# Decays loaded to every partition by their own transfer, and eight blank products in one run, at the start of a linear-attention and mixer kernel

## The chip, the cores and the metric

The kernel runs on one core of one Trainium2 chip. The metric is device time in microseconds for the whole program, the median of three runs. The profile is of one further execution of the same program; its span, from the first instruction to the last, is about one microsecond shorter than the measured time.

## What is computed

Two blocks follow each other. The first is linear attention with a decay per head: batch 4, 8 heads, 768 positions, head size 64, in blocks of positions.

```python
rel = pos[:, None] - pos[None, :]
Dmask = np.where(rel >= 0, lam[:, None, None] ** rel[None, :, :], 0.0)
for b in range(nb):
    intra = einsum('bhic,bhjc->bhij', qb, kb) * Dmask[None]
    intra = einsum('bhij,bhjd->bhid', intra, vb)
    inter = einsum('bhid,bhde->bhie', qb * lam_pow[None], kv_state)
    out[:, :, sl] = intra + inter
    kv_state = lam_block * kv_state + einsum('bhsd,bhse->bhde', kb * rev_pow, vb)
```

Everything that depends on the decays (`Dmask`, `lam_pow`, `rev_pow`, `lam_block`) is made from the eight numbers `lam`.

The second block takes the attention output as x (4 x 768 x 512), mixes positions through a product of rank 32, and applies a two-layer network of width 2048:

```python
h = xt @ U @ V
u = x + h.transpose(0, 2, 1)
ch = np.maximum(u @ w_ch1, 0.0) @ w_ch2
return u + ch
```

## The kernel before

The work is tiled by 128 positions: 24 tiles (four batches of six), called s in the code. The kernel uses its own block of 128 positions where the reference has 64, which gives the same result.

**The front**, about the first 115 us, goes through the tiles one after the other. The order is written out by hand: the list `pieces` names, for each tile, functions that each emit a few instructions, and the loop at the end of the set-up calls them in that order. An engine executes its instructions in the order in which they are emitted, so the list is also the order on every engine. For a tile these are:

- `prep`: TensorE transposes q and k (line 348) by a product with the identity, and ScalarE copies the result out of PSUM (line 351). For tile 0 this goes in two halves, q then k, and the first halves use the PSUM tags pq and pk, the second ones pt and pu. Afterwards `load_next` issues a later load of q and of k.
- `scale`: GpSimd multiplies q by powers of the decay (`powq`) and the next tile's k by `rev`.
- `scores`: TensorE multiplies q by k into PSUM tile `pss` (line 393), 16 passes.
- `masked`: VectorE multiplies `pss` by the decay mask into `sm` (line 402), two instructions.
- `inter` and `intra`: TensorE multiplies the state and the masked scores by v into `px` (lines 434 and 446); ScalarE copies `px` out.
- `state`: TensorE and VectorE update the running state (line 411 and after), and the next v is loaded.
- later ones for the mixer's rank-32 product (`low`, `mix`) and the transposes of its result (`turn`), and `aside`, which converts the weights.

The loads of q, k and v (line 272) come from HBM in rows of 256 B. A tile of each is 256 KB; three buffers hold q and v, four hold k. Almost all are issued by SyncE in the order of the calls; only the two halves of the first k are on ScalarE's queue. Tile 0's q and k come in two halves each.

**The hidden layers** follow, from about 115 us to the end: `hidden` (lines 722 and 732) and `product` (lines 855 to 859), long runs of 128x512 products with conversions on the other engines beside them.

**The set-up**, which the change touches, lies before the loop. `blank` is a tile of zeros. `keep_busy(n)` (line 336) makes n products of `blank` with itself, which nobody reads, into PSUM with tag pq. A product in fp32 is two passes of TensorE, each with its weight load. `lam_row` holds the eight decays and 128 ones on one partition. The product `pl` (line 670) of the ones and the decays puts the decays on all 128 partitions, and VectorE copies it into `lamb` (line 672). From `lamb`, `constants` makes the mask with eight scans (line 302) and `powers` makes `powq` with four (line 314); `rev` is a column of the mask (line 675). VectorE executes these in that order, and `masked(0)` after them.

The tile names in the profile are those of the code: `idle` is the output of the blank products, `pl` that of the ones product, `qraw`, `kraw` and `vraw` are loads.

Of the kernel before, what the change touches and what calls it, by code (L numbers as in the profile page):

```python
# [8 lines left out]
FP32 = mybir.dt.float32  # L9
# [5 lines left out]
P = 128  # L15
# [3 lines left out]
def kernel(  # L19
# [28 lines left out]
    nc = tc.nc  # L48

    B, H, S, D = q.shape  # L50
# [37 lines left out]
    def set_ends(t):  # L88
        nc.vector.memset(t[:, 0:1], 1151.0)
        nc.vector.memset(t[:, 1:2], 255.0 * (1 << 23))  # L90
        ends.append(t)
# [145 lines left out]
    consts = att_ctx.enter_context(tc.tile_pool(name="consts", bufs=1))  # L237
# [10 lines left out]
    def one_bank(shape, name, tag):  # L248
        return psf.tile(shape, FP32, tag=tag, name=name)
# [7 lines left out]
    lamb = consts.tile([P, H], FP32, name="lamb")  # L257
# [40 lines left out]
    def constants():  # L298
        for a in range(HP):
            for x in range(2):  # L300
                h = 2 * a + x
                nc.vector.tensor_tensor_scan(
                    mask[:, x, a, :], lamb[:, h : h + 1].broadcast_to([P, P]), ident, 0.0,
                    ALU.mult, ALU.add,
                )
# [26 lines left out]
    def keep_busy(n):  # L332

        out = one_bank([P, C], "idle", "pq")
        for i in range(n):
            nc.tensor.matmul(out=out[:, 0:P], lhsT=blank, rhs=blank, start=True, stop=True)  # L336
# [240 lines left out]
    def load_next(name, engine=nc.sync):  # L577
        if waiting[name]:
            load(name, waiting[name].pop(0), engine)
# [71 lines left out]

    ordered = ctx.enter_context(ExitStack())
    ordered.enter_context(tc.manual_schedule())
    lam_row = consts.tile([1, H + P], FP32, name="lam_row")
    blank = x_pool.tile([P, C], FP32, tag="x", name="blank")[:, 0:P]
    nc.vector.memset(blank, 0.0)
    nc.vector.memset(lam_row[:, H:], 1.0)
    set_ends(vp[:, S + C : S + C + 2].bitcast(FP32))
    nc.scalar.dma_start(out=lam_row[:, 0:H], in_=lam.unsqueeze(0))
    load_next("q", nc.sync)  # L660
    load_next("k", nc.scalar)
    for name in "qkvkv":
# [2 lines left out]
    for name in "qkv":  # L665
        load_next(name)
    make_identity(nc, ident)
    keep_busy(2)
    pl = one_bank([P, H], "pl", "pt")
    nc.tensor.matmul(out=pl, lhsT=lam_row[:, H:], rhs=lam_row[:, 0:H], start=True, stop=True)  # L670
    keep_busy(3)
    nc.vector.tensor_copy(out=lamb, in_=pl)
    constants()
    powers()
    nc.vector.tensor_copy(out=rev, in_=mask[:, :, :, P - 1])
# [282 lines left out]
```

## Time and profile before

| | |
|---|---|
| time, median of three (lowest, highest) | 673.5 us (673.49, 673.6) |
| span of the profile | 672.5 us |
| TensorE products busy | 665.9 us, 99% of the span |
| VectorE busy | 496.6 us, 74% |
| ScalarE busy | 278.7 us, 41% |
| GpSimd busy | 112.8 us, 17% |
| mean rate of the transfers | 195 GB/s; 208 to 239 GB/s in each of the first six of 40 slices |
| blank products, ten passes | 2.9 us busy, 1.05 to 4.38 us |
| scans for the mask, eight | 2.6 us busy, 0.40 us each |

How to read the lines shown later: in the chain of work and the timeline each line begins with the start in us and the duration in us, then the engine. "x6" is six instructions merged into one line, and the duration is that from the first start to the last end. In brackets stands how long the engine had been idle before, and what ended it. A busy TensorE is not a TensorE at its full rate: the same product can take twice as long at half the clock. SPq and ACTq are the queues on which SyncE and ScalarE issue transfers; the duration there is that of issuing, not of the transfer.

### The profile page before, as it was taken

How to read it: one execution, taken by the hardware profiler on the slowest of the kernel's cores; microseconds unless marked ns; L12 is line 12 of the kernel's file. 1: busy time of each engine (PE TensorE's matmuls, PEld its weight loads, DVE VectorE, ACT ScalarE, POOL GpSimd, SP SyncE). 2: the span in 40 equal slices, each digit the busy share in tenths (PEclk: the TensorE clock that was granted, in tenths of full speed). 3: DMA queues.
4: the chain of work that ended last, by engine and by line, in shares of the span. 5: the costliest groups of instructions: out<-in, count | busy, mean ns of one | idle time of the engine just before them, and what ended most of it. 6: DMA issues, size and time to landing. Idle time of an engine off the chain costs nothing.

```text
span 672.5 us, 13170 instructions
## 1 busy us (share of the span) xinstructions
PE 665.9 (99%) x5124; PEld 545.4 (81%) x5124; DVE 496.6 (74%) x873; ACT 278.7 (41%) x517; POOL 112.8 (17%) x92
## 2 busy tenths in 40 slices
PE   9999999999999999999999999999999999999997
PEld 8888898787888888888888888888888888888885
DVE  4679999777999777777797255786586775865854
ACT  4675767454555444444455121332232322322320
POOL 4455667340000000000000000030030200300300
PEclk9999999999999999999999999999999999999999
DMA  9999993264776555555587999854363363443421
GB/s 208 214 228 239 237 232 109 84 215 156 235 276 240 204 203 204 204 203 204 203 280 253 325 314 387 291 185 140 94 206 107 110 204 94 158 155 95 161 89 62
DMA packets 131775, 131.27 MB, mean 195 GB/s; under 512 B 81346, under 2 KB 89794, under 8 KB 131714
## 3 DMA queue, kind: packets, MB, share of 16 engines
q1 hardware_dynamic: 130656, 130.18, 61.3%
q8 instruction: 40, 0.66, 0.4%
q10 hardware_dynamic: 1058, 0.26, 0.2%
q14 instruction: 21, 0.17, 0.1%
HBM read 80.09 MB, written 50.33 MB: 194 GB/s over the span
## 4 chain that ended last, share of the span: by engine, by line
PE 96%; DVE 2%; ACT 2%; issue 0%; DVEq 0%; ACTq 0%
PE pz L722 27%; PE pz L857 13%; PE pd L732 13%; PE pz L855 13%; PE pd L859 13%; PE pss L393 3%; PE px L446 3%; PE put L523 2%; PE pq L348 2%; PE px L434 1%; PE pkv L411 1%; PE pk L348 1%; PE pp L461 1%; PE pu L506 1%; PE idle L336 0%; ACT qt L351 0%
## 5 line engine op out<-in xcount | busy, mean ns | idle before, releaser
L722 PE MATMUL pz<-u_hl,w 128*128 128x512 f32 x768 | 190.4, 397 | 0.0
L722 PEld LDWEIGHTS pz<-u_hl,w 128*128 128x128 f32 x768 | 144.0, 188 | 35.5 <-issue 0.4
L857 PE MATMUL pz<-w_hl,m 128*128 128x512 f32 x384 | 151.1, 396 | 0.0
L855 PE MATMUL pz<-w_hl,m 128*128 128x512 f32 x384 | 150.9, 396 | 0.0
L859 PE MATMUL pd<-w_d,m 128*128 128x512 f32 x384 | 149.5, 396 | 0.0
L838 ACT ACTIVATE m<-mt 128x512 fp32r<-128x512 f32 x96 | 60.7, 633 | 196.0 <-PE pd L859 141.7
L839 DVE SCALAR_TENSOR_TENSOR m<-rm,m 128x512 fp32r<-128x512 f32 x96 | 71.4, 745 | 52.2 <-ACT m L838 52.1
L884 POOL TENSOR_TENSOR o<-o,u 128x512 f32<-128x512 f32 x20 | 29.9, 1529 | 447.3 <-DVE o L880 447.3
L737 DVE SCALAR_TENSOR_TENSOR r<-pd,r 128x512 f32<-128x512 f32 x96 | 61.8, 685 | 54.0 <-ACT r L728 43.5
L732 PE MATMUL pd<-u_d,w 128*128 128x512 f32 x384 | 98.6, 397 | 0.0
L728 ACT ACTIVATE r<-pz 128x512 f32<-128x512 f32 x96 | 52.2, 596 | 93.6 <-PE pz L722 92.9
L857 PEld LDWEIGHTS pz<-w_hl,m 128*128 128x128 f32 x384 | 72.3, 188 | 17.7
L855 PEld LDWEIGHTS pz<-w_hl,m 128*128 128x128 f32 x384 | 72.3, 188 | 17.6
L859 PEld LDWEIGHTS pd<-w_d,m 128*128 128x128 f32 x384 | 72.3, 188 | 17.6
L732 PEld LDWEIGHTS pd<-u_d,w 128*128 128x128 f32 x384 | 72.1, 188 | 17.3
L840 DVE SCALAR_TENSOR_TENSOR m<-m 128x512 fp32r<-128x512 f32 x96 | 69.0, 720 | 0.9
L837 DVE TENSOR_SCALAR mt<-rm 128x512 uint32<-128x512 uint32 x96 | 46.1, 481 | 28.0 <-DMA rm<-r_d 27.6
L402 DVE TENSOR_TENSOR sm<-pss,mask 128x512 f32<-128x512 f32 x48 | 30.8, 683 | 7.4 <-PE pss L393 7.3
L205 ACT CAST w<-wt 128x512 fp32r<-128x512 f32 x32 | 19.9, 622 | 30.5 <-DVE wt L202 23.4
L376 POOL TENSOR_TENSOR qs<-qt,powq 128x512 f32<-128x512 f32 x20 | 25.9, 1296 | 23.3 <-ACT qt L351 22.3
L446 PEld LDWEIGHTS px<-vraw,sm 128*64 128x64 f32 x768 | 24.7, 137 | 6.0 <-issue 2.4
L446 PE MATMUL px<-vraw,sm 128*64 128x64 f32 x768 | 28.3, 226 | 0.5 <-DVE sm L402 0.4
(88 smaller groups left out, 682.7 us busy)
## 6 DMA issues: line engine op xcount, KB each, us to landing
r_d<-r SPq DMA_DIRECT2D x96, 256.0 KB, 2.5
rm<-r_d SPq DMA_DIRECT2D x96, 256.0 KB, 2.7
words<-in_moe_w_ch_dram SPq DMA_DIRECT2D x30, 512.0 KB, 4.4
w_d<-w SPq DMA_DIRECT2D x16, 768.0 KB, 3.3
w_hl<-w_d SPq DMA_DIRECT2D x16, 512.0 KB, 6.2
vraw<-in_v_dram SPq DMA_DIRECT2D x24, 256.0 KB, 4.6
u_d<-x_nat SPq DMA_DIRECT2D x24, 256.0 KB, 3.5
u<-u_d SPq DMA_DIRECT2D x24, 256.0 KB, 4.1
```

Source lines behind the costliest of these rows:

```text
L446: nc.tensor.matmul(out=px[half[t], x, a, :], lhsT=sm[:, x, a, half[t]], rhs=vr[:, 2 * a + x, :], start=(first and a == 0), stop=(a == HP - 1),
L722: nc.tensor.matmul(out=acc[g][0], lhsT=w[:, n, ct, :], rhs=uhl[g][:, n, ct, :], start=(ct == 0 and n == 0), stop=(ct == CT - 1 and n == 1),)
L728: nc.scalar.mul(rs[g], acc[g][0], 4096.0 + 1.0)
L732: nc.tensor.matmul(out=acc[g][1], lhsT=w[:, 2, ct, :], rhs=ud[g][:, ct, :], start=(ct == 0), stop=(ct == CT - 1),)
L737: nc.vector.scalar_tensor_tensor(rs[g], acc[g][1], 4096.0, rs[g], ALU.mult, ALU.add)
L837: nc.vector.tensor_scalar(t.bitcast(U32), r.bitcast(U32), HI, None, ALU.bitwise_and)
L838: nc.scalar.activation(out=m[:, 0], in_=t, func=AF.Relu)
L839: nc.vector.scalar_tensor_tensor(m[:, 1], r, 0.0, hi, ALU.max, ALU.subtract)
L840: nc.vector.scalar_tensor_tensor(m[:, 2], hi, E, low, ALU.mult, ALU.subtract)
L855: nc.tensor.matmul(out=pz, lhsT=m[:, 0, cols], rhs=hl[:, 0], start=first, stop=False)
L857: nc.tensor.matmul(out=pz, lhsT=m[:, 1, cols], rhs=hl[:, 1], start=False, stop=end)
L859: nc.tensor.matmul(out=pd, lhsT=m[:, 2, cols], rhs=dd, start=first, stop=end)
```

## The change

The decays are sent to all 128 partitions by the transfer itself, which reads the eight numbers once for each partition and writes them straight into `lamb`. The tile `lam_row`, the filling of its ones, the product `pl` and the copy out of PSUM go. The blank products were two, then the ones product, then three; they become eight in one run. What they are for is to keep TensorE at work from its first microsecond until the first data are there. Nothing else is edited; the order of the loads is as before.

```diff
     ordered.enter_context(tc.manual_schedule())
-    lam_row = consts.tile([1, H + P], FP32, name="lam_row")
     blank = x_pool.tile([P, C], FP32, tag="x", name="blank")[:, 0:P]
     nc.vector.memset(blank, 0.0)
-    nc.vector.memset(lam_row[:, H:], 1.0)
     set_ends(vp[:, S + C : S + C + 2].bitcast(FP32))
-    nc.scalar.dma_start(out=lam_row[:, 0:H], in_=lam.unsqueeze(0))
+    nc.scalar.dma_start(out=lamb, in_=lam.unsqueeze(0).broadcast_to([P, H]))
     load_next("q", nc.sync)
     load_next("k", nc.scalar)
...
     make_identity(nc, ident)
-    keep_busy(2)
-    pl = one_bank([P, H], "pl", "pt")
-    nc.tensor.matmul(out=pl, lhsT=lam_row[:, H:], rhs=lam_row[:, 0:H], start=True, stop=True)
-    keep_busy(3)
-    nc.vector.tensor_copy(out=lamb, in_=pl)
+    keep_busy(8)
     constants()
     powers()
     nc.vector.tensor_copy(out=rev, in_=mask[:, :, :, P - 1])
```

## The prediction

> **What bounds the kernel now.** I read the page first: busy shares, the slices, the chain that ended last.
>
> ```profile
> DMA  9999993264776555555587999854363363443421
> ...
> PE 96%; DVE 2%; ACT 2%; issue 0%; DVEq 0%; ACTq 0%
> ```
>
> The chain is TensorE nearly everywhere, and the list of waits between 110 us and the end shows only nine waits of TensorE, the longest 0.4 us. So a shift of TensorE's work at the start should reach the end almost unchanged, unless something in the front takes it back. The slices name the candidate: the DMA engines are full in the first six slices, about 100 us. Next, the chain in order of time for the first microseconds:
>
> ```profile
> 0.83 0.18 DVE blank L656
> ...
> 1.05 1.23 PE idle L336 x4
> 2.28 0.52 PE pl L670 x2
> 2.80 1.58 PE idle L336 x6
> 4.38 0.10 issue
> 4.48 0.66 PE pq L348 x2
> ...
> 6.42 2.01 PE pss L393 x16
> ...
> 11.32 1.09 PE pss L393 x16
> ```
>
> The blanks and the ones product fill TensorE to 4.38; the first transposes follow 0.10 us later. Each fp32 blank is two passes (five blanks are ten passes). The first scores take 2.01 us, the second, same shapes, 1.09: the first ran at half the rate. The single pass starts show where this changes: start to start a 128-column pass takes 0.21 us up to 8.85 us and 0.11 us after. The trace's record of the granted clock begins its full interval at 8.885 us and ends it at 671.07: 662.19 us, which is 194 times 3.413. Then the timeline of the start, where VectorE and the loads can be seen:
>
> ```profile
> 2.83 0.17 DVE L672 COPY lamb<-pl 128x8 f32<-128x8 f32 x1 [1.69 <-PE pl L670]
> 3.11 2.63 DVE L302 TENSOR_TENSOR_SCAN mask<-lamb,ident 128x128 f32<-128x128 f32 x8
> ...
> 7.33 0.14 DVE L675 COPY small<-mask 128x8 f32<-128x8 f32 x1
> ...
> 8.48 1.29 DVE L402 TENSOR_TENSOR sm<-pss,mask 128x512 f32<-128x512 f32 x2 [1.01 <-PE pss L393]
> ```
>
> VectorE has its constants at 7.47 and waits 1.01 us for the scores: the decays are not what sets the pace. The scores are.
>
> **What the Trainium skill says.** "TensorE: Matmul & The Clock Gate", Part 1 (the HAM clock gate): TensorE starts at half its clock and gets the full one only after a busy window of about 3.4 us, counted in windows that run freely. The trace agrees: halves before 8.885, full after, and 194 whole windows of 3.413 us. "DMA: Bandwidth & Descriptors"[...]. Here the 32 bytes of lam, issued at 0.73, landed at 1.92 by the semaphore record, and the first q half (128 KB, same issue time) 2.4 us after issue. The same page, on the semaphore's 16 counts: a transfer over 128 partitions runs on 16 engines and counts as landed with the last. The record of landings has 16 for each such load, the last up to 1.3 us after the rest.
>
> **The change, part by part.**
>
> The decays' transfer. One packet of 32 B becomes 128, eight for each engine; here a 32 B packet took 7 ns and a 256 B one 15 to 18, so the packets are nothing and the latency is all. It is issued at 0.73 as now, between 1.92 (the small load) and 3.13 (last landing of the first q half). I take 2.5. The k halves behind it on the queue land perhaps 0.05 us later; their slack (0.34 us) covers that.
>
> VectorE loses a 0.17 us memset, and the copy at 2.83; its scans wait for the transfer instead of the product. All that is queued behind that wait is the scans, the powers, rev and the first masking. From 3.11 to 7.47 this is 4.36 us of work, so rev is done at 2.5 + 4.36 = 6.9 instead of 7.47 (6.5 to 7.5 from the two ends). GpSimd's key scaling, which waits for rev, comes at about 6.9; nobody waits for it before 10.6. So this part is worth nothing by itself, but the constants stay ahead of scores that come earlier.
>
> TensorE. 1.23 us for four passes and 1.65 us for six (the timeline's value for the second group, 2.73 to 4.38) give 0.21 us a pass. Sixteen in one run are 1.23 + 12 x 0.213 = 3.79 us: 1.05 to 4.84. The first transpose waits for the last blank, since both use tag pq, and its semaphore wait is seen to end only with it; so it starts at 4.84 + 0.10 = 4.94, not 4.48. That is a loss of 0.46 us, and the q half (landed 3.13) is ready anyway.
>
> The clock. In the position of the windows in this trace they end at 2.06, 5.47 and 8.885. In 2.06 to 5.47 the kernel before has a product with eight columns, a gap before the transposes, and 38% of the window filled with blank passes (66% with the transposes): not enough. The window that did release the clock was filled to 50% (86% with transposes), counting 0.213 us a pass and the scores' pairs of passes, which start together, once. After the change blanks alone fill 2.06 to 4.63, 75% (91% with transposes). By either count it is fuller than the one that sufficed, so I expect the full clock at 5.47. Transposes then start at 4.94, 5.18, 5.39 and after that every 0.11 us, the last at 5.98 (6.00 now). ScalarE copies the four halves, 0.37 us each, some 0.3 us apart when nothing holds them: the last goes from 6.45 to 6.82. Scores start at 6.25, wait for that copy at the middle, and finish for VectorE at about 7.5, where 8.48 stands now; the warm run of scores is 1.21 us from start to masking (11.25 to 12.46) against 2.13 now. Gain at the masking: 1.0 us, and the attention output follows it by the same distance as now.
>
> The loads. They do not come sooner. SyncE's queue is without a gap to 25 us and the engines are full, so TensorE running 1.0 us ahead uses up slack:
>
> ```profile
> 21.15 1.20 SPq L272 DMA_DIRECT2D vraw<-in_v_dram  x1
> ...
> 27.23 1.15 PE L446 MATMUL px<-vraw,sm 128*64 128x64 f32 x32
> ...
> vraw<-in_v_dram SPq DMA_DIRECT2D x1, 256.0 KB, 5.3
> ```
>
> This v tile (s = 4) lands at 21.15 + 5.3 = 26.45 and is used at 27.23: 0.78 us of slack. The q tile of s = 3 (issued 10.89, 5.4 us to landing, used 17.26) has 0.99, the v of s = 3 (16.27, 5.7, 22.94) 0.98; all others up to 60 us have over 1.2, and growing, except the first tile's halves. So 0.2 to 0.3 us of the gain is given back by 27 us: 0.78 less 0.05 for the semaphore leaves 0.7 us. After that the kernel runs as before, earlier. 673.5 - 0.7 = **672.8**.
>
> **Rivals.**
> - *The loads come along* (the last engine's lag of up to 1.3 us falls elsewhere): the whole 1.0 us stays, 672.5. For it: in that v load 15 of 16 engines are done at 25.2. Against it: three loads in a row show such a lag.
> - *The clock comes earlier still*, the timed runs having another window position: at the full clock before 4.5 us the transposes of tile 0 end with the last k half (5.23) and not at 6.2, 0.5 us more, 1.5 in all if the loads give way too: 672.0. Against: the three times lie within 0.11 us, which does not look like a wandering window.
> - *No earlier clock* (zeros do not count as activity, or the window wants more): the 0.46 us of blanks is lost in front of everything and the clock still comes at 8.885: 673.95, slower than before.
> - *The wait for the broadcast takes the product's place*: masking starts at landing + 4.36, so anything past 4.1 us is a loss. If 128 reads of one address land only with the second k half (5.23), masking is at 9.6, 1.1 us late: 674.6; at 6 us it is 675.4. For it: every first load is in flight then. Against: those, 512 packets each, are in by 3.1 to 5.2.
>
> **How the numbers follow.** 0.48 for the forecast (672.8), 0.14 for loads that come along, 0.14 for the early clock, 0.14 for no earlier clock, 0.10 for a late broadcast. The range leaves out half of the early clock and most of the late broadcast, 0.15 together: 672.1 to 674.2. 0.2% is 1.35 us: faster than 672.15 only in the early-clock case, 0.14; slower than 674.85 in a little over half of the late-broadcast case, 0.06; the rest, 0.80, is within.
>
> **What would show it.** Blanks in one group ending near 4.84 and first transposes at 4.94; scores of tile 0 in some 1.2 us and not 2.0; the masking at 7.5; scans starting at 2.3 to 3.0; then short waits of TensorE for q at 16.3 and for v at 22.0 and 26.5, and the second step's work 0.7 us ahead from 27 us to the end. I am wrong if the scores of tile 0 still take 2 us (clock), if the scans start after 4 us (transfer), or if waits later in the front, which this trace does not have, eat the rest.

## The result and the profile after

| | before | after |
|---|---|---|
| time, median (lowest, highest) | 674.0 us (673.49, 675.5) | 677.92 us (677.26, 678.62) |
| ratio to before, 95% interval | | 1.0054 (1.0039 to 1.0068) |
| span of the profile | 672.5 us | 676.7 us |

The kernel became slower by about 3.9 us. The figure for before includes three further runs made beside the changed kernel, which took 674.39 to 675.5 us. The three on which the forecast stood (673.49 to 673.6) lie at the low end of what this kernel shows: on the four chips of the experiments, in 20 to 55 runs each, its median is 674.5 to 675.0. Against those runs, on the chip where the changed kernel ran again, its loss is 2.5 us. Line numbers of the changed kernel lie lower than those of the kernel before, by six behind the last removed line.

The page of the kernel after, the busy share of the DMA engines in 40 slices and the chain that ended last:

```profile
DMA  9999997154777655555567999855363363453431
...
PE 88%; DVE 4%; DMA 3%; SPq 2%; ACT 2%; issue 0%; DVEq 0%; ACTq 0%
```

The engines are full in the same first six slices, but the chain, which was 96% TensorE, now has 5% in transfers and in the queue that issues them. The start of the timeline of the kernel after:

```profile
0.73 0.45 ACTq L657 DMA_DIRECT2D lamb<-in_lam_dram  x1
...
1.05 3.78 PE L336 MATMUL idle<-blank 128*128 128x128 f32 x16 [1.05 <-DVE blank L655]
...
4.35 2.63 DVE L302 TENSOR_TENSOR_SCAN mask<-lamb,ident 128x128 f32<-128x128 f32 x8 [3.34 <-DMA lamb<-in_lam_dram]
...
4.94 0.57 PE L348 MATMUL pq<-ident,qraw 128*128 128x128 f32 x2
...
7.50 0.44 PE L348 MATMUL pk<-ident,kraw 128*128 128x128 f32 x2 [1.15 <-DMA kraw<-in_k_dram]
7.87 1.25 PE L393 MATMUL pss<-qt,kt 64*128 64x128 f32 x16
...
9.16 1.29 DVE L402 TENSOR_TENSOR sm<-pss,mask 128x512 f32<-128x512 f32 x2 [0.45 <-PE pss L393]
```

TensorE does what the prediction said: sixteen passes to 4.83, the first transposes at 4.94, tile 0's scores in 1.25 us. The record of the granted clock has the full clock from 5.285 us; it was 8.885. But the decays are there only at 4.35, and the second k half, which landed at 5.23, now lands at 7.46 (record of landings). The masking comes at 9.16 and not at 7.5. It waited for the scores, and these for the second k half. Among the waits of TensorE in the first 40 us are three rows that the kernel before does not have:

```profile
PE px L446 <- DMA vraw<-in_v_dram: 1.8, 2, 1.1
PE pk L348 <- DMA kraw<-in_k_dram: 1.3, 2, 1.1
...
PE pq L348 <- DMA qraw<-in_q_dram: 0.6, 1, 0.6
```

All three are loads. The view of the transfers between 6 and 14 us shows why: first before, then after. In each fence the first line is what all queues moved, the second SyncE's queue alone (packets, MB, time that its packets took as a share of 16 engines' time).

```profile
DMA packets 7856, 2.00 MB, mean 250 GB/s; under 512 B 7855, under 2 KB 7855, under 8 KB 7855
...
q1 hardware_dynamic: 7855, 1.98, 109.2%
```

```profile
DMA packets 6841, 1.74 MB, mean 217 GB/s; under 512 B 6840, under 2 KB 6840, under 8 KB 6840
...
q1 hardware_dynamic: 6635, 1.67, 124.1%
```

Long after the transfer of the decays is over, the same packets of 256 B take longer. Before, 109.2% of 16 engines' 8 us are 139.8 us for 7855 packets, 17.8 ns each; after, 158.8 us for 6635 packets, 23.9 ns each. At 13% less data per microsecond, the loads, whose slack was 0.3 us for the first k and 0.8 to 1.0 us for the tightest of the later ones, set the pace. The experiments had to find where these 6 ns come from.

### The profile page after: what moved, and what is told of

Read it like the earlier page. It is cut to its first block, busy times and chain, and to the rows that moved or that the text cites. A ratio compares the mean times of both kernels' runs of the same rounds, so it can differ in the third digit from the quotient of the medians.

```text
span 676.7 us, 13173 instructions
## 1 busy us (share of the span) xinstructions
PE 665.6 (98%) x5128; PEld 544.6 (80%) x5128; DVE 498.1 (74%) x871; ACT 278.0 (41%) x517; POOL 112.4 (17%) x92
## 4 chain that ended last, share of the span: by engine, by line
PE 88%; DVE 4%; DMA 3%; SPq 2%; ACT 2%; issue 0%; DVEq 0%; ACTq 0%
PE pz L716 27%; PE pz L851 13%; PE pz L849 13%; PE pd L726 13%; PE pd L853 13%; PE px L446 2%; PE pss L393 2%; DMA qraw<-in_q_dram 1%; SPq L272 1%; PE put L523 1%; DVE sm L402 1%; PE pp L461 1%; DMA vraw<-in_v_dram 1%; PE pkv L411 1%; DMA u_d<-x_nat 1%; PE pq L348 1%
## 5 line engine op out<-in xcount | busy, mean ns | idle before, releaser
L205 ACT CAST w<-wt 128x512 fp32r<-128x512 f32 x32 | 19.9, 621 | 30.6 <-DVE wt L202 23.4
```

## The experiments

The ratios below are to the kernel before on the same chip. How far they can be trusted is shown by the first run: the unchanged kernel, against itself, came out at 0.9985 (0.9978 to 0.9993), 673.55 against 674.9 us. Differences under 0.2% are therefore not taken as shown, even where an interval excludes 1.

### The parts apart

The kernel before again, on the chip of the next three:

> The kernel before, unchanged, on the chip of the next three runs. If the chip makes the loads slow (rival), its first packets of 256 B take more than 20 ns each here too, its v load of s = 4 lands after 28 us, and the span is 674 us or more. If the transfer does it (theory), packets take 15 to 18 ns as in the first profile, that load lands near 26.5 us and the span is near 672.5 us.

673.55 us, span 672.0. Its packets took 18 ns throughout, the v load of s = 4 landed at 25.5. So the chip is not what made the packets slow.

Blanks alone:

```diff
-    keep_busy(3)
+    keep_busy(6)
```

> Three more blanks behind the ones product (2, product, 6), decays by the old way. Theory that the transfer alone costs: same or faster by up to 0.8 us, scores of tile 0 in 1.2 us, first loads as before, transposes from about 5.5 us. Rival that the blanks cost (0.46 us later transposes, given on to the end): slower by 0.5 to 1.5 us.

Ratio 0.999 (0.998 to 1.0): no loss of the size in question. Against the run just above it is 0.55 us slower (674.1 against 673.55), too little to count as shown, but the traces have it too: masking is at 8.92 instead of 8.48, and the work stays 0.44 us behind to the end. The loads were at their old rate (249 GB/s from 6 to 14 us). The full clock was granted at 7.73, and the scores, though in 1.25 us, started late:

```profile
7.62 1.25 PE L393 MATMUL pss<-qt,kt 64*128 64x128 f32 x16
```

Decays by their transfer, with five blanks, the number of the kernel before; the edit is to the changed kernel:

```diff
-    keep_busy(8)
+    keep_busy(5)
```

> Decays sent by their transfer, five blanks as before, no ones product. Theory that the transfer delays every load behind it: slower by as much as the whole change, 2.5 to 4 us, first k halves landing 1.3 us and more after those of the kernel before. Rival that the blanks or the earlier clock cost: same time as before, within 0.5 us.

Ratio 1.0033 (1.0026 to 1.004), 2.1 us, a little less than expected; the k halves landed 0.9 and 1.1 us later than in the unchanged kernel of this group, not 1.3. This half of the change carries the loss. Its transfers from 6 to 14 us:

```profile
DMA packets 6874, 1.75 MB, mean 219 GB/s; under 512 B 6873, under 2 KB 6873, under 8 KB 6873
...
q1 hardware_dynamic: 6873, 1.73, 125.4%
```

That is 23.4 ns a packet (125.4% of 16 engines' 8 us, over 6873), as in the changed kernel, and without its blanks. The changed kernel once more beside it:

> The changed kernel, unchanged, on the same chip. If the chip had a part in the first comparison, the difference to the kernel before is smaller here, 1 to 3 us; if not, 3.5 to 4.5 us.

Ratio 1.0035 (1.0023 to 1.0047), the same as with the transfer alone. Its 2.5 us fall in the range that was to mean that the chip had a part. They don't show that: the changed kernel took as long as at first (677.39 and 677.92), and what differs is the kernel before (674.9 here, 673.55 in the run above, 674.0 at first). On this chip the two traces, changed kernel against the kernel before, can be laid over each other. The products `px` of tiles 0 to 5 start later by 0.38, 1.31, 1.77, 2.47, 2.73 and 2.88 us; nothing is added up to tile 12; tile 13 stands at 3.76, and the last product of the kernel at 3.67. The second step is in ScalarE's waits between 40 and 95 us of the changed kernel, where the kernel before has no such row:

```profile
ACT x_nat L451 <- DMA u_d<-x_nat: 4.3, 2, 3.1
```

ScalarE waits for a buffer whose contents must first be stored, and the store stands in the same late queue of transfers. The longer of the two waits (3.14 us) ends at 71.74; TensorE's next product (L434), which waited for ScalarE, starts at 72.43, and tile 13's `px` at 75.22 instead of 71.47.

### Is it the transfer?

The next three keep the decays' old way and add one transfer of 128 packets of 32 B into a tile that nobody reads:

```diff
+    spare = consts.tile([P, H], FP32, name="spare")
     nc.scalar.dma_start(out=lam_row[:, 0:H], in_=lam.unsqueeze(0))
+    nc.scalar.dma_start(out=spare, in_=lam.unsqueeze(0).broadcast_to([P, H]))
```

> The kernel before, and one more transfer of lam's 32 bytes to 128 partitions of a tile that nobody reads, behind lam's own small load and ahead of the k halves. Theory that the transfer itself is the cost, whoever reads it: slower by 2 to 3 us, under 300 KB moved in the first 4 us (400 without it), packets of 256 B at 22 to 25 ns from 5 to 16 us. Rival that the late decays (scans from 4.35 us) are the cost: same time as before, since here the decays come by the old way at 3.1 us.

Ratio 1.0041 (1.0026 to 1.0055), packets at 24 to 26 ns from 6 us on. So it does not matter that the decays come later. With 128 addresses instead of one (`in_=q[0, 0, 0:P, 0:H]`):

> The same spare transfer, 128 packets of 32 bytes, but each read from another address (the first 8 numbers of 128 rows of q). If reading one address 128 times is what takes long: its packets start within about 0.5 us instead of 1.8, and the time is that of before within 0.5 us. If 128 small packets or small writes are the cost: slower by 2 to 3 us, like the run with one address.

Ratio 1.0031 (1.0019 to 1.0042). Half of the expectation came true: the small packets started within 0.5 us (2.30 to 2.80) and not within 1.7 us (2.45 to 4.20), and 396 KB were moved in the first 4 us instead of 268. The other half failed: it was as slow, and its packets of 256 B took 25 ns by 6 us. Behind the k halves:

> The spare transfer of lam to 128 partitions behind the two k halves on ScalarE's queue instead of ahead of them. If its place ahead of the first loads is the cost: the first q and k halves land as before (k by 5.3 us) and the time is within 0.7 us of before. If it leaves the engines out of step wherever it stands: packets at 22 to 25 ns for some 10 us after it, slower by 1 to 2.5 us.

Ratio 1.0027 (1.0017 to 1.0038): the first 4 us as before (405 KB), slow packets all the same. By now it looked as if any small transfer left the engines out of step. A second try at the blanks, with five behind the product, ran in this group:

> Two blanks, the ones product, five blanks (two more than before); decays by the old way. If the full clock comes a window earlier through this, scores of tile 0 in 1.2 us and 0.3 to 0.8 us faster than before; if the gap round the product keeps the window from counting, scores in 2.0 us and within 0.4 us of before.

Ratio 1.0001 (0.999 to 1.0012). The clock came at 7.23, scores took 1.25 us from 7.21 and the masking was at 8.50, within a few hundredths of the kernel before. Two more blanks were worth nothing here.

### The place of the buffers

All slow kernels had one more thing in common, which no view of the profile shows; it follows from the order and the sizes of the tiles, and the built program has it as the tiles' addresses. The tile pools lay tiles one behind the other in a partition. In the kernel before, `lamb`, `small`, `mask`, `powq` and `lam_row` (136 numbers, 544 bytes) end at byte 121600, and there the first q buffer starts: a multiple of 256, and all buffers of q, k and v follow in steps of 2048. Without `lam_row` it starts at 121056, 224 bytes past a multiple of 256; with the 32-byte spare tile at 121632, 32 bytes past. A row of 256 B then lies across a multiple of 256. Nearly all packets of 256 B are rows of q, k and v (73728 of 74496; the rest are the rows of the mixer's U), so slow packets of this size point to these buffers. To test this, no transfer is needed:

```diff
-    lam_row = consts.tile([1, H + P], FP32, name="lam_row")
+    lam_row = consts.tile([1, H + P + 8], FP32, name="lam_row")[:, 0 : H + P]
```

> The kernel before with eight unused numbers more in lam_row: no transfer is added or removed, but the buffers of q, k and v start 32 bytes further on in each partition, 32 past a multiple of 64, where all kernels with slow packets so far had them. Theory of place: packets of 256 B at 22 to 26 ns from 5 to 16 us, under 2600 KB moved in the first 14 us, slower by 2 to 2.5 us. Rival, that a transfer of small packets puts the engines out of step: packets at 18 ns and the time of before.

Ratio 1.0033 (1.002 to 1.0046), transfers from 6 to 14 us:

```profile
DMA packets 6700, 1.70 MB, mean 213 GB/s; under 512 B 6699, under 2 KB 6699, under 8 KB 6699
...
q1 hardware_dynamic: 6699, 1.69, 111.6%
```

21.3 ns a packet. Thirty-two unused bytes cost as much as the whole change. The engines' work on the moved tiles is no slower (ScalarE's first copies take 0.37 us and VectorE's scans for `powq` 1.37, as before), so it is the loads that suffer. With sixteen numbers (64 bytes) and with sixty-four (256 bytes) in place of eight:

> The same with sixteen numbers more: the buffers of q, k and v move by 64 bytes and stay on a multiple of 64 (no longer of 256). If a multiple of 64 is what counts: packets at 18 ns and the time of before within 0.5 us. If a multiple of 256 counts: slow like the shift by 32.

```profile
DMA packets 6799, 1.73 MB, mean 216 GB/s; under 512 B 6798, under 2 KB 6798, under 8 KB 6798
...
q1 hardware_dynamic: 6798, 1.71, 119.9%
```

Ratio 1.0024 (1.0016 to 1.0031), 22.6 ns a packet.

> The kernel before with 64 unused numbers more in lam_row: the buffers of q, k and v move by 256 bytes and stay on a multiple of 256 (now also of 512). If rows of 256 B that straddle a multiple of 256 are what makes packets slow: packets at 18 ns and the time of before within 0.5 us. If any move of the buffers costs: 1.5 to 2.5 us slower like the moves by 32 and 64.

```profile
DMA packets 7206, 1.83 MB, mean 229 GB/s; under 512 B 7205, under 2 KB 7205, under 8 KB 7205
...
q1 hardware_dynamic: 7205, 1.81, 100.5%
```

Ratio 0.9996 (0.9987 to 1.0005), 17.9 ns a packet. Here the engines had idle stretches, which lowers the rate and not the packets' pace. So a multiple of 64 is not enough, a multiple of 256 is, and a move as such costs nothing. A move by 128 was not run.

It is the run of displaced rows that is slow, not each row by itself. U's 768 rows go to a tile in another pool, which does not move and lies 224 bytes past a multiple of 256 in every kernel. By their place in SyncE's queue, their packets took 18.0 ns in the kernel before, among the rows of q, k and v on the multiple, and 23.6 ns in the changed kernel, among displaced ones.

The Trainium skill, "DMA: Bandwidth & Descriptors", How a descriptor splits into AXI transactions, says that a run of bytes is read in pieces of up to 256 B, each of which must start on a multiple of 256; by that rule a row of 256 B that starts elsewhere needs two pieces instead of one. That agrees with the slow runs, as far as it goes: the page speaks of reading and gives no price for a destination in a partition, which is what was moved here.

The counterpart is the changed kernel with its place restored:

```diff
-    lamb = consts.tile([P, H], FP32, name="lamb")
+    lamb = consts.tile([P, 2 * H], FP32, name="lamb")[:, 0:H]
```

> The changed kernel with lamb taken from a tile twice as wide, so that the buffers of q, k and v start on a multiple of 64 again (of 256, as in the kernel before). Theory of place: packets at 18 ns, v of s = 4 landed by 27 us, 2 us faster than the changed kernel; against the kernel before between 0.7 us faster (the prediction) and 1 us slower, the transfer of the decays costing what the 140 KB less moved in the first 4 us take, some 0.6 us. Rival of small packets: still 2.5 to 3 us slower than before.

Ratio 0.9992 (0.9984 to 0.9999), 673.93 us: 0.43% or 2.9 us less than the changed kernel's 1.0035. Its transfers from 6 to 14 us and its timeline:

```profile
DMA packets 7856, 2.00 MB, mean 249 GB/s; under 512 B 7855, under 2 KB 7855, under 8 KB 7855
...
q1 hardware_dynamic: 7855, 1.98, 109.4%
```

```profile
4.26 2.63 DVE L302 TENSOR_TENSOR_SCAN mask<-lamb,ident 128x128 f32<-128x128 f32 x8 [3.25 <-DMA lamb<-in_lam_dram]
...
6.46 1.25 PE L393 MATMUL pss<-qt,kt 64*128 64x128 f32 x16
...
8.54 1.28 DVE L402 TENSOR_TENSOR sm<-pss,mask 128x512 f32<-128x512 f32 x2
```

The packets are back at 17.8 ns. The scores are done at 7.7, but the masking starts at 8.54, straight behind VectorE's own work, with no wait in brackets: the scans began at 4.26. The early clock is there (the scores of the kernel before are done at 8.43), and the late decays take it back: the masking of the kernel before starts at 8.48. Whether this kernel beats the kernel before is not settled: 0.08% is less than the unchanged kernel differed from itself.

### What the transfer costs with the place kept

> The kernel before with the spare transfer of lam to 128 partitions ahead of the k halves, its tile 64 bytes wide so that the buffers of q, k and v stay on a multiple of 64. What is left of its cost is that of reading one address 128 times ahead of the first loads: k halves 1.3 us later, slower than before by 0.5 to 1.2 us. Theory of small packets: slower by 2 to 3 us as with the 32-byte tile.

The edit is the first spare transfer with a tile of 64 bytes. It measured 1.0034 (1.0021 to 1.0047), but it moved the buffers by 64, which the run beside it showed to be slow by itself. It decides nothing. With a tile of 256 bytes:

> The kernel before with the spare transfer of lam to 128 partitions, its tile 256 bytes wide, so that the buffers of q, k and v move by 256 bytes as in the run beside it. What the transfer costs with the place kept: some 150 KB less moved in the first 4 us, k halves 1 us later, and with the slack of the loads 0.3 to 1.2 us slower than before, packets at 18 ns. If small packets slow the later ones after all: packets at 23 ns and 2 to 3 us slower.

Ratio 1.0013 (1.0007 to 1.002), packets at 18 ns; the k halves land at 5.42 and 6.72 (4.47 and 5.49 in the unchanged kernel of the first group), and 266 KB were moved in 4 us. The nearest control is e4_shift_256, on the same chip and with the same move but without the transfer: 674.56 against 675.69 us, k halves at 4.66 and 5.38. So the transfer costs about 1.1 us here, as expected, and its masking stands at 9.51 where the kernel before has 8.48. The difference is 0.17%, within what two copies of one kernel have differed, so its size is an estimate.

The changed kernel with the place kept and five blanks:

> Decays sent by their transfer with five blanks, the tile of the decays widened so that the buffers keep their multiple of 256: the changed kernel so widened, with three blanks fewer. If the three blanks bring the earlier clock and this is worth something: slower than the padded changed kernel by 0.5 to 1 us, so 0 to 0.7 us slower than before, scores of tile 0 in 2 us. If the loads set the pace whatever the clock: as fast as that one, 0.5 us faster than before.

Ratio 1.0011 (1.0004 to 1.0017); full clock at 8.69, scores in 2.08 us, masking at 8.70. Between this run and the widened changed kernel lie the three blanks: 1.0011 against 0.9992, with masking at 8.70 and 8.54. But the profiled executions of the two, 673.92 and 673.89 us, end within 0.03 us of each other. The gain of the three blanks, too, is at the limit of what these runs can tell.

## Why the prediction was wrong

It forecast 672.8 us, range 672.1 to 674.2, from a chain of steps. Those on TensorE came true. Two failed: the tile that was taken away was put at nothing, and the decays' transfer was put at too little.

**The blanks: right.** Sixteen passes to 4.83 and first transposes at 4.94, as worked out.

**The clock: right in kind, its moment in part luck.** Full from 5.285 (5.47 forecast), scores in 1.25 us. The sum took over the windows' position from one trace, but they stand elsewhere in each execution. With sixteen passes in one run the grant came at 4.34, 5.29 and 6.08; with the product among more blanks at 7.73 and 7.23; with TensorE's work as in the kernel before at 8.89 and 8.80, but also at 6.72, and in e2_spare_late at 6.07. So a long run of blanks makes an early grant likelier, and an early one can come without it. That three times within 0.11 us do "not look like a wandering window" was wrong: three were too few, and 55 runs of the same kernel spread from 672.93 to 676.62. What an earlier clock is worth shows in e4_shift_256: grant at 6.72, masking at 7.72, and from tile 1 to the end the work stands 0.7 us ahead of the trace of e1_before_again. That equals the forecast gain by chance: the masking came 0.76 us sooner there and not 1.0, and nearly nothing was given back.

**The decays' transfer: mis-sized.** "So the packets are nothing and the latency is all", landing at 2.5 us. Its packets took 7 to 9 ns each, as assumed, but they started over 1.8 us, from 2.06 to 3.88, and the last landed at 4.25. With 128 different addresses they started within 0.5 us, so it is reading one address 128 times that takes long. Constants were done at 8.72 and not 6.9. "Their slack (0.34 us) covers that" failed with it: the k halves came 1.3 and 2.2 us later, not 0.05, and the scores, so the masking, waited for the second. Part of this is the place of the buffers: with it kept (e3_after_padded) they land at 5.12 and 6.05, still some 0.8 us later than in the kernel before. The rival of the late broadcast had this shape and was given one chance in ten. By its own sum, landing + 4.36, the landing at 4.25 puts the masking at 8.6, a loss of 0.13 us; its 674.6 supposed a landing at 5.23, which did not come. With the place kept, such a transfer cost about 1.1 us, so it is not where most of the loss comes from.

**The removed tile: the step that is missing, and the one that decided.** The prediction costed the removed memset, the removed product and the removed copy, and took the removed tile for nothing. Removing 544 bytes moved every buffer behind them off a multiple of 256. Shown by three pairs: 32 and 64 unused bytes made the kernel before slower by 0.33% and 0.24% without any other edit, 256 did not, and 32 bytes given back to the changed kernel made up 2.9 us. With the place kept the changed kernel stands at 0.9992, near the forecast's 672.8 / 673.5 = 0.9990. That does not confirm the forecast's path: the masking starts at 8.54 and not at 7.5, and from tile 1 on its work stands 0.05 to 0.24 us behind the trace of e1_before_again.

**The loads: right in kind.** "They do not come sooner" and "uses up slack" hold, and three waits were named by tile: q at 18.85, v at 25.3 and 30.3 follow their landings within about 0.1 us. The waits for the two k halves and for q at 14.36 were not named. What was forecast as a give-back of 0.3 us became the whole loss, because the loads were later, not only no sooner. The waits for stores near tile 13, 0.9 us, were not foreseen.

What stays open: why rows across a multiple of 256 are slow in a run and not singly (what was shown is that buffers of q, k and v placed 32, 64 or 224 bytes past the multiple slow the loads), and whether a multiple of 128 would do. Also, whether the widened changed kernel is faster than the kernel before.

## What to carry to other kernels

A tile's size is part of an edit: before costing a removed or added tile at nothing, work out where the buffers behind it come to lie, and keep the buffers that take most of the loads on a multiple of 256 when they are filled in rows of 256 B. When, as here, loads have less than a microsecond of slack and the engines are full, ask of every edit what it does to the loads' rate, not only to their order. And a spare tile without a transfer is a control that a suspected transfer needs, because adding a transfer adds its tile too.

## What the runs showed of the hardware that was not expected

- With the buffers of q, k and v displaced, so that their rows lie across a multiple of 256, the packets of 256 B from 6 to 14 us took 21 to 25 ns on average, against 17.8 ns on the multiple, and the rate fell from 250 GB/s to between 211 and 219. U's packets, displaced in every kernel, took 18.0 ns in the kernel before.
- The extra time is not always there. In the changed kernel packets took 17.8 ns in the first 4 us and 18.4 from 18 to 20 us, in the same displaced buffers. How busy the engines are does not decide it alone: from 18 to 20 us they were full (102%), and from 22 to 24 us, at 42%, packets took 21.6 ns.
- 128 reads of the same 32 B started over 1.7 to 2.0 us (1.5 behind the k halves), some 12 to 16 ns apart; 128 reads of 32 B at different addresses over 0.5 us.
- The windows that grant the clock stand at another place in each execution: full clock at 8.89, 8.80 and 6.72 us in kernels whose TensorE work was the same up to then.
- Transposes fill such a window. In e1_blanks_alone the last 3.413 us before the grant (4.31 to 7.73) were filled to about 36% without transposes and to 86% with them; the 3.413 us before that, filled to about 69% by blanks and the product, brought no grant. (Counted from the starts of the passes, 0.213 us each.)
